# Splitting weights on GpSimd, one run of k times v matmuls, and a new order of issue in a fused mLSTM and MoE kernel

## The chip, the cores and the metric

The kernel runs on one core of a Trainium2 chip. The metric is the device time of one execution in microseconds. Times of a kernel are given as the median of several runs. One execution was taken by the hardware profiler; the rows below are from that one.

## What is computed

Two parts follow one another. The first is an mLSTM layer (4 batches, 8 heads, 768 time steps, head size 40), a recurrence with gates:

```python
m_new = np.maximum(f_gate[:, :, t] + m, i_gate[:, :, t])
f_stab = np.exp(f_gate[:, :, t] + m - m_new)
i_stab = np.exp(i_gate[:, :, t] - m_new)
C = f_stab[:, :, None, None] * C + i_stab[:, :, None, None] * np.einsum('bhd,bhe->bhde', vt, kt)
n = f_stab[:, :, None] * n + i_stab[:, :, None] * kt
h_tilde = np.einsum('bhde,bhe->bhd', C, qt)
denom = np.maximum(np.abs(nq), 1.0)
y[:, :, t] = o * h_tilde / denom
```

Its output, 3072 tokens of 320 values, goes through an MLP with 2048 hidden units: `h = x @ w_in`, `g = h * erf(softplus(h))`, `g @ w_out`. Inputs and output are float32; the two weights reach the chip as 64 bit numbers, of which the kernel makes float32 values itself.

## The kernel before

**Attention.** The sequence is cut into 6 chunks of 128 tokens. A step is one chunk of one batch, so there are 24 steps. Within a step the recurrence is written as matrices: decay factors (`pe`, then `ex` on ScalarE and a triangular select `sel` on GpSimd), scores of q and k (`S`, TensorE), their product `w` (VectorE), the output `ph` from scores, v and the state, and the update of the state: `vg` (v times a decay, VectorE), `pk` (k times `vg`, TensorE, lines 635 to 639), `sa` and `sk` (VectorE, or ScalarE in the first chunk). Heads are held as four pairs; even heads (j = 0) lie on partitions 0 to 39, odd heads (j = 1) on 64 to 103. `pk` is made once for each j, four matmuls each, into a PSUM tile of its own; the last chunk has none, so 20 steps have it. `y` (line 669) is the step's output; its last 64 columns are doubled (line 672) so that three transposes (`tr`) of 128 columns bring tokens onto columns; `xh` and `xl` are its high and low part in the fp32r type that TensorE reads in one pass.

**MLP.** Two batches of a chunk (256 tokens) are a block, and a block has four groups of 512 hidden units, so there are 48 groups. A group has 32 matmuls `up` (line 818), the activation on ScalarE and VectorE over tiles of 128x1024 (`hb`, `a`, `b`, `w` and others), its high and low part `gh` and `gl` (lines 868, 873), and 24 matmuls `dn` (lines 887, 888, 890) into two PSUM banks.

**Weights.** They are decoded in the start of the program, in 26 pieces: 16 of w_out with 320 columns, and 10 of w_in with 512, two of which cover the tail rows. For each, `val` (ScalarE, line 707) and `bits` (VectorE, three instructions, lines 712 to 715) make the float32 value in the tile `bits`, of which there are two, `hi` (ScalarE, line 720) rounds it to the high part, `dif` (TensorE, lines 725 and 726) forms value minus high part in PSUM with an identity and a negative identity, and `lo` (ScalarE, line 730) writes that as the low part.

**What sets the order.** Every piece of work is put into a list with a due time: the time of its unit (a step, a group, a decode) plus an offset from a table by the name of the part. The list is sorted by these numbers and issued in that order, so that each engine gets its instructions in the order of the list. All loads and stores are issued on SP. The tile pools hold few buffers (four PSUM tiles for attention, `dif` among their users), so an instruction also waits for the release of a buffer.

Of the kernel before, what the change touches and what calls it, by code (L numbers as in the profile page):

```python
# [9 lines left out]
F32 = mybir.dt.float32  # L10
F32R = mybir.dt.float32r
# [38 lines left out]
SETUP = {'setup': -653.6399, 'rhs0': -316.5197, 'rhs1': -7.8928, 'sel': -20.425}  # L50
GATE = {'load': -160.6071,
    'scan': -129.7377,
    'g': -118.9644,
    'sum': -85.9459,
    'exp': -69.3145,
    'part0': -64.8632,
    'part1': -57.829,
    'part2': -53.3066,
    'rhs': -44.557}
ATT_FIRST = {'load': -98.3436,  # L60
    'loadv': -167.9076,
    'khi': -0.958,
    'qhi': -84.1108,
    'klo': -36.0204,
    'qlo': -40.8927,
    'stk0': -106.1734,
    'stk1': -42.28,
    'rows': -205.5,
    'pe0': -204.9951,
    'pe1': -84.7223,  # L70
    'ex0': -104.2074,
    'ex1': -80.6796,
    'sel0': -99.9161,
    'sel1': -76.6928,
    'S0': -72.5713,
    'S1': -66.4977,
    'vg0': -86.1606,
    'vg1': -75.2945,
    'w0': -66.7387,
    'w1': -60.3516,  # L80
    'th': -51.6975,
    'pq': -84.6914,
    'qa': -69.7526,
    'ph0': -50.833,
    'ph1': -48.4014,
    'ph2': -41.1641,
    'ph3': -34.4417,
    'pk0': -76.6612,
    'pk1': -43.5318,
    'sa0': -34.523,  # L90
    'sa1': -33.2596,
    'sk0': -75.5148,
    'sk1': -41.374,
    'den': -25.7622,
    'yg': -25.29,
    'y': -21.6911,
    'tr': -15.7542,
    'xh': -3.4201,
    'xl': -0.3588}
ATT_NEXT = {'load': -108.5865,  # L100
    'loadv': -65.7264,
    'khi': -43.9486,
    'qhi': -36.8481,
    'klo': 33.0974,
    'qlo': 4.1048,
    'stk0': -62.7653,
    'stk1': 33.0459,
    'rows': -112.0,
    'pe0': -92.4353,
    'pe1': -82.6231,  # L110
    'ex0': -85.3469,
    'ex1': -74.7973,
    'sel0': -83.8594,
    'sel1': -59.1013,
    'S0': -64.4044,
    'S1': -29.3249,
    'vg0': -46.0099,
    'vg1': -19.402,
    'w0': -39.4592,
    'w1': -14.1493,  # L120
    'th': -41.0893,
    'pq': -109.6295,
    'qa': -38.5364,
    'ph0': -10.0541,
    'ph1': -6.3375,
    'ph2': 5.1946,
    'ph3': 6.4602,
    'pk0': -35.9301,
    'pk1': -7.3506,
# [853 lines left out]
```

## Time and profile before

| | us |
|---|---|
| median of 3 runs | 543.33 |
| lowest and highest run | 537.8, 544.72 |
| the profiled execution | 542.79 |
| its span, first to last instruction | 541.1 |

The span is what the profile can show; 1.7 us of the execution lie outside it. Engines are called PE (TensorE), PEld (its weight loads), DVE (VectorE), ACT (ScalarE), POOL (GpSimd) and SP (which issues DMAs). A row of the instructions in order of time has the start, the duration, engine, line, operation and tiles; matmuls are pipelined, so that durations overlap and the distance from one start to the next is what a matmul costs. An fp32 matmul is recorded as two.

### The profile page before, as it was taken

What the parts mean: (1) busy time and instruction counts of PE and PEld (TensorE: products, weight loads), DVE (VectorE), ACT (ScalarE), POOL (GpSimd) and SP (SyncE); (2) the same over time, 40 slices, a digit from 0 to 9 for tenths busy, and PEclk for the clock granted to TensorE, in tenths of its full rate; (3) what the DMA queues carried; (4) which work ended last, traced back from release to release, by engine and by line L of the source; (5) the groups of instructions that cost most, each with busy time, mean ns of one, the idle gap of its engine ahead of it and who ended that gap; (6) DMA issues with size and microseconds to landing.
All of it is one profiled execution on the core that took longest, in us unless ns stands there. A gap on an engine that the chain in (4) does not pass through costs nothing.

```text
span 541.1 us, 10846 instructions
## 1 busy us (share of the span) xinstructions
PE 521.8 (96%) x4086; PEld 491.9 (91%) x4086; DVE 435.9 (81%) x693; ACT 448.2 (83%) x714; POOL 92.4 (17%) x112
## 2 busy tenths in 40 slices
PE   3989999999899999999999999999999999999997
PEld 2757799899899999999999999999999999999986
DVE  5987899979788878888888898788898678776663
ACT  5776999989868978979878978878979889889993
POOL 3220001312211211211211211211211220200000
PEclk9996999999899999999999999999999999999999
DMA  8996114504504503404513504513504514400000
GB/s 272 276 324 214 40 34 134 153 27 144 150 2 152 165 25 124 150 16 152 155 35 116 157 17 138 166 38 106 167 8 135 162 44 137 140 1 26 0 25 24
DMA packets 28302, 58.85 MB, mean 109 GB/s; under 512 B 4156, under 2 KB 8764, under 8 KB 28252
## 3 DMA queue, kind: packets, MB, share of 16 engines
q1 hardware_dynamic: 28252, 58.18, 34.8%
q8 instruction: 32, 0.52, 0.4%
q14 instruction: 18, 0.15, 0.1%
HBM read 33.40 MB, written 3.93 MB: 69 GB/s over the span
## 4 chain that ended last, share of the span: by engine, by line
PE 84%; DMA 6%; DVE 4%; ACT 3%; issue 1%; SPq 1%; POOL 0%; DVEq 0%; ACTq 0%; POOLq 0%
PE h L818 32%; PE po L887 10%; PE po L890 10%; PE po L888 9%; PE pa L629 7%; DMA n<-in_w_in_dram 4%; PE pa L626 4%; PE pa L586 3%; PE pa L639 3%; PE pa L725 2%; DMA stk<-parts 2%; PE pa L566 2%; PE pa L678 1%; PE pa L589 1%; SPq L554 1%
## 5 line engine op out<-in xcount | busy, mean ns | idle before, releaser
L818 PE MATMUL h<-xh,wh 128*128 128x256 f32 x576 | 160.1, 287 | 0.0
L818 PE MATMUL h<-xl,wh 128*128 128x256 f32 x576 | 157.3, 282 | 0.0
L887 PE MATMUL po<-woh,gh 128*128 128x320 f32 x384 | 122.4, 330 | 2.1 <-ACT o_sb L896 1.3
L888 PE MATMUL po<-wol,gh 128*128 128x320 f32 x384 | 114.9, 310 | 0.0
L818 PEld LDWEIGHTS h<-xh,wh 128*128 128x128 f32 x576 | 109.6, 190 | 1.9 <-issue 1.0
L818 PEld LDWEIGHTS h<-xl,wh 128*128 128x128 f32 x576 | 109.5, 190 | 0.2
L818 PE MATMUL h<-xh,wl 128*128 128x256 f32 x384 | 108.3, 282 | 0.0
L873 DVE TENSOR_TENSOR gl<-hb,gh 128x1024 fp32r<-128x1024 f32 x48 | 59.7, 1243 | 21.8 <-ACT gh L868 16.6
L577 POOL TENSOR_SCALAR_AFFINE_SELECT dm<-dm 128x512 f32<-128x512 f32 x48 | 47.2, 985 | 170.2 <-ACT dm L573 162.2
L887 PEld LDWEIGHTS po<-woh,gh 128*128 128x128 f32 x384 | 72.8, 190 | 2.7 <-ACT o_sb L896 1.6
L868 ACT ACTIVATE gh<-hb 128x1024 fp32r<-128x1024 f32 x48 | 50.9, 1060 | 28.3 <-DVE hb L863 27.8
L888 PEld LDWEIGHTS po<-wol,gh 128*128 128x128 f32 x384 | 72.9, 190 | 0.6
L818 PEld LDWEIGHTS h<-xh,wl 128*128 128x128 f32 x384 | 73.0, 190 | 0.0
L890 PE MATMUL po<-woh,gl 128*128 128x320 f32 x384 | 72.6, 319 | 0.0
L855 DVE SCALAR_TENSOR_TENSOR n<-n,n 128x1024 f32<-128x1024 f32 x48 | 58.7, 1224 | 14.9 <-ACT n L847 12.2
L851 DVE SCALAR_TENSOR_TENSOR n<-n,hb 128x1024 f32<-128x1024 f32 x48 | 61.8, 1288 | 4.3 <-ACT n L842 4.2
L863 DVE SCALAR_TENSOR_TENSOR hb<-n,hb 128x1024 f32<-128x1024 f32 x48 | 58.4, 1217 | 7.6 <-ACT n L859 7.4
L828 ACT ACTIVATE hb<-h 128x512 f32<-128x512 f32 x96 | 57.3, 597 | 6.1 <-PE h L818 3.3
L859 ACT ACTIVATE n<-n 128x1024 f32<-128x1024 f32 x48 | 51.4, 1070 | 11.4 <-DVE n L855 11.3
L890 PEld LDWEIGHTS po<-woh,gl 128*128 128x128 f32 x384 | 58.9, 188 | 1.1
L834 ACT ACTIVATE n<-h 128x512 f32<-128x512 f32 x96 | 57.8, 602 | 0.0
L629 PE MATMUL pa<-kvo,dm 128*128 128x41 f32 x384 | 54.8, 273 | 0.0
(102 smaller groups left out, 896.4 us busy)
## 6 DMA issues: line engine op xcount, KB each, us to landing
stk<-parts SPq DMA_DIRECT2D x120, 160.0 KB
kvo<-in_kvo_dram SPq DMA_DIRECT2D x24, 484.0 KB
parts<-in_w_out_dram SPq DMA_DIRECT2D x5, 960.0 KB
parts<-in_qk_dram SPq DMA_DIRECT2D x20, 208.0 KB
q_t<-in_qk_dram SPq DMA_DIRECT2D x20, 208.0 KB
out_dram<-o_sb SPq DMA_DIRECT2D x24, 160.0 KB
stk<-in_qk_dram SPq DMA_DIRECT2D x4, 416.0 KB
hb<-in_w_in_dram SPq DMA_DIRECT2D x2, 512.0 KB
```

The lines of the kernel that those rows point to most:

```text
L629: nc.tensor.matmul(v.ph[:, 2 * p + j], v.w[j][:, p], v.v1[:, 2 * p + j], start=(c == 0), stop=(c == 0 or j == 1))
L818: nc.tensor.matmul(v.h[n // 2][:, n % 2 * T:(n % 2 + 1) * T], w, m, start=(q == 0), stop=(q == len(ops) - 1))
L828: nc.scalar.activation(v.hb[:, hs], v.h[i], AF.Copy)
L834: nc.scalar.activation(v.a[:, hs], v.h[i], AF.Tanh, scale=PARAMS[0], bias=PARAMS[1])
L851: nc.vector.scalar_tensor_tensor(out=v.a, in0=v.a, scalar=PARAMS[8], in1=v.hb, op0=ALU.add, op1=ALU.mult)
L855: nc.vector.scalar_tensor_tensor(out=v.a, in0=v.a, scalar=PARAMS[9], in1=v.b, op0=ALU.mult, op1=ALU.add)
L859: nc.scalar.activation(v.a, v.a, AF.Tanh, scale=PARAMS[10], bias=PARAMS[11])
L863: nc.vector.scalar_tensor_tensor(out=v.hb, in0=v.a, scalar=1.0, in1=v.hb, op0=ALU.add, op1=ALU.mult)
L873: nc.vector.tensor_tensor(v.gl, v.hb, v.gh.bitcast(F32), op=ALU.subtract)
L887: nc.tensor.matmul(po[k, b], v.gh[:, ts], woh[:, w], start=(j == 0), stop=False)
L888: nc.tensor.matmul(po[k, b], v.gh[:, ts], wol[:, w], start=False, stop=False)
L890: nc.tensor.matmul(po[k, b], v.gl[:, ts], woh[:, w], start=False, stop=(j == NFF - 1))
```

## The change

Four edits:

- `dif` is gone, with the negative identity and one PSUM tile per decode; the low part is a subtraction on GpSimd, from the value and the high part, both in SBUF.
- `pk` is one part instead of two: eight matmuls, even and odd heads in turn, into one PSUM tile. The sums into the state read their rows of it.
- The copy that doubles y's last 64 columns moves from GpSimd to VectorE.
- Nearly all due times have other values. Two lines of the tables as they are now, as an example:

```diff
-    'klo': -21.0673,
+    'klo': -21.0991,
-    'pk0': 6.9497,
-    'pk1': -1.5624,
+    'pk': -0.9185,
```

The code:

```diff
-        nc.scalar.activation(nident, ident, AF.Copy, scale=-1.0)
...
+        if not last:
+
+            @at('pk')
+            def _():
+                v.pk = psum(NPR, V1)
+                for p in range(NPR):
+                    for j in range(2):
+                        nc.tensor.matmul(v.pk[64 * j:64 * j + D, p], v.kn[:, 2 * p + j], v.vg[j][:, p], start=True, stop=True)
+
         for j in range(0 if last else 2):
             js = slice(64 * j, 64 * j + D)
-
-            @at(f'pk{j}')
-            def _(j=j, js=js):
-                v.pk[j] = pk = psum(NPR, V1)
-                for p in range(NPR):
-                    nc.tensor.matmul(pk[js, p], v.kn[:, 2 * p + j], v.vg[j][:, p], start=True, stop=True)
...
-                    nc.scalar.activation(so, v.pk[j][js], AF.Copy)
+                    nc.scalar.activation(so, v.pk[js], AF.Copy)
                 else:
-                    nc.vector.tensor_tensor(so, so, v.pk[j][js], op=ALU.add)
+                    nc.vector.tensor_tensor(so, so, v.pk[js], op=ALU.add)
...
-            nc.gpsimd.tensor_copy(y[:, 320:384], y[:, 256:320])
+            nc.vector.tensor_copy(y[:, 320:384], y[:, 256:320])
...
-        @at('dif')
-        def _():
-            v.z = ps_a.tile([128, 512], F32, name="pa")[:, 0:n]
-            nc.tensor.matmul(v.z, ident, v.val, start=True, stop=False)
-            nc.tensor.matmul(v.z, nident, hi(), start=False, stop=True)
-
         @at('lo')
         def _():
-            nc.scalar.activation(lo(), v.z, AF.Copy)
+            nc.gpsimd.tensor_tensor(lo(), v.val, hi().bitcast(F32), op=ALU.subtract)
```

What the new order does is shown at three places. The first is TensorE ahead of the first `up` matmul. Before, with transposes at line 678, scores at 589, `dif` at 725 and 726, `up` at 818:

```order
L678 MATMUL pa<-ident,kvo 128x128 x3
L589 MATMUL pa<-stk 128x128 x4
L725 MATMUL pa<-bits,ident 128x512
L726 MATMUL pa<-wh,nident 128x512
L589 MATMUL pa<-stk 128x128 x4
L725 MATMUL pa<-bits,ident 128x512
L726 MATMUL pa<-wh,nident 128x512
L818 MATMUL h<-xh,wh 128x256
```

The same place now, where the transposes are line 682, the last decay matmuls 569 and `up` 816:

```order
L569 LDWEIGHTS rhsE_77
L569 MATMUL pa<-splB_83,rhsE_77 128x128
L682 MATMUL pa<-ident,kvo 128x128 x6
L816 MATMUL h<-xh,wh 128x256
L816 MATMUL h<-xl,wh 128x256
```

The eight score matmuls of the third batch, and the decode's, no longer stand between the transposes and the first `up`; the scores come behind the first group of 32 `up` matmuls.

The second place is GpSimd behind its set-up, where line 559 copies decay rows for a batch, 577 is the select and 672 the copy of y. Before:

```order
L559 COPY splB_81<-spl 32x256
L559 COPY splB_82<-spl 32x256
L577 AFFINE_SELECT dm<-dm 128x512 x4
L559 COPY splB_83<-spl 32x256
L559 COPY splB_84<-spl 32x256
L672 COPY kvo<-kvo 128x64
L577 AFFINE_SELECT dm<-dm 128x512 x2
```

Now, with the subtractions at line 728:

```order
L560 COPY splB_80<-spl 32x256
L560 COPY splB_81<-spl 32x256
L728 TENSOR_TENSOR wol<-bits,woh 128x320 x2
L560 COPY splB_82<-spl 32x256
L560 COPY splB_83<-spl 32x256
L728 TENSOR_TENSOR wol<-bits,woh 128x320 x2
L578 AFFINE_SELECT dm<-dm 128x512 x2
L728 TENSOR_TENSOR wol<-bits,woh 128x320
L578 AFFINE_SELECT dm<-dm 128x512 x2
L728 TENSOR_TENSOR wol<-bits,woh 128x320
L728 TENSOR_TENSOR wl<-bits,wh 128x512 x2
```

Four subtractions now stand ahead of the first select, and five ahead of the third and fourth.

The third place is SP's list of loads, where `gt` is the gates of a chunk (here the second chunk's), `parts` raw w_out, and `hb`, `gh`, `gl` and `n` raw w_in. Before:

```order
L748 DMA n_328<-in_w_in_dram 128x1024
L519 DMA stk<-in_qk_dram 104x1024 x2
L748 DMA gh<-in_w_in_dram 128x1024
L775 DMA wh<-stk 64x512 x4
L429 DMA gt<-in_gates_dram 128x2x128
L525 DMA kvo<-in_kvo_dram 128x968 x2
```

Now:

```order
L746 DMA gh<-in_w_in_dram 128x1024
L746 DMA hb<-in_w_in_dram 128x1024
L430 DMA gt<-in_gates_dram 128x2x128
L761 DMA n_286<-in_w_in_dram 64x1024 x2
L786 DMA parts<-in_w_out_dram 128x3x640
L746 DMA n_324<-in_w_in_dram 128x1024
```

The gate load has moved from behind most loads of weights to right behind the first two of w_in.

## Rows read from the trace of the kernel before

**Rows 1.** Busy time of each engine, share of the span, instructions.

```profile
PE 521.8 (96%) x4086; PEld 491.9 (91%) x4086; DVE 435.9 (81%) x693; ACT 448.2 (83%) x714; POOL 92.4 (17%) x112
```

**Rows 2.** Stretches: us, busy us and (instructions) by engine, clock, DMA share, GB/s.

```profile
48.00:60.00 12.00, 12.00 (x76) 9.66 (x75) 8.43 (x19) 9.44 (x20) 0.00 (x0) 0.86 0.23 80
60.00:110.00 50.00, 48.80 (x376) 45.71 (x376) 47.31 (x81) 47.91 (x83) 6.98 (x8) 1.00 0.32 95
...
200.00:300.00 100.00, 100.00 (x828) 97.11 (x827) 84.75 (x138) 83.91 (x129) 18.75 (x19) 1.00 0.34 105
```

**Rows 3.** Groups of instructions: shapes, count | busy us, mean ns | idle before.

```profile
L639 PEld LDWEIGHTS pa<-vg,kvo 128*40 128x40 f32 x320 | 15.3, 117 | 6.9 <-issue 3.6 <-DVE gl L873 0.7 <-DVE dm L600 0.6
L595 DVE TENSOR_TENSOR vg<-kvo,dm 128x164 f32<-128x164 f32 x40 | 14.0, 352 | 0.0
...
L726 PE MATMUL pa<-woh,nident 128*128 128x320 f32 x16 | 8.9, 556 | 0.0
...
L726 PE MATMUL pa<-wh,nident 128*128 128x512 f32 x8 | 7.3, 913 | 0.0
...
L726 PE MATMUL pa<-stk,nident 128*128 128x512 f32 x2 | 1.5, 742 | 0.0
```

**Rows 4.** TensorE in order of time, two decodes between up matmuls.

```profile
51.53 0.70 PE L725 MATMUL pa<-bits,ident 128*128 128x320 f32 x2
...
52.22 0.28 PE L818 MATMUL h<-xh,wh 128*128 128x256 f32 x1
...
60.83 1.02 PE L725 MATMUL pa<-bits,ident 128*128 128x512 f32 x2
...
61.92 0.28 PE L818 MATMUL h<-xh,wh 128*128 128x256 f32 x1
```

**Rows 5.** TensorE: first and last decode ahead of the first up matmul.

```profile
10.37 1.38 PE L725 MATMUL pa<-bits,ident 128*128 128x320 f32 x2
...
45.96 2.07 PE L725 MATMUL pa<-bits,ident 128*128 128x512 f32 x2
...
48.25 0.41 PE L818 MATMUL h<-xh,wh 128*128 128x256 f32 x1
```

**Rows 6.** TensorE: four score matmuls and what follows.

```profile
58.71 1.16 PE L589 MATMUL pa<-stk 40*128 40x128 f32 x8
59.79 0.38 PE L818 MATMUL h<-xh,wh 128*128 128x256 f32 x1
```

**Rows 7.** Waits of VectorE, 0 to 48 us: total, times, longest.

```profile
DVE bits L712 <- ACT bits L707: 4.0, 5, 1.7
DVE m_c L435 <- DMA gt<-in_gates_dram: 3.9, 2, 2.1
```

**Rows 8.** GpSimd in order of time, 35 to 38 us.

```profile
35.10 0.80 POOL L577 TENSOR_SCALAR_AFFINE_SELECT dm<-dm 128x512 f32<-128x512 f32 x1 [0.40 <-ACT dm L573]
37.55 0.24 POOL L672 COPY kvo<-kvo 128x64 f32<-128x64 f32 x1 [1.65 <-DVE kvo L669]
37.73 0.64 POOL L577 TENSOR_SCALAR_AFFINE_SELECT dm<-dm 128x512 f32<-128x512 f32 x1
```

**Rows 9.** VectorE in order of time: beside that select, and the third gl.

```profile
34.91 0.49 DVE L713 SCALAR_TENSOR_TENSOR bits<-parts,bits 128x320 int32<-128x320 int32 x1
35.44 0.80 DVE L715 SCALAR_TENSOR_TENSOR bits<-parts,bits 128x320 int32<-128x320 int32 x1
...
93.90 1.23 DVE L873 TENSOR_TENSOR gl<-hb,gh 128x1024 fp32r<-128x1024 f32 x1 [0.46 <-ACT gh L868]
```

**Rows 10.** TensorE: its first matmul with the third gl.

```profile
96.69 0.45 PE L890 MATMUL po<-woh,gl 128*128 128x320 f32 x2
```

**Rows 11.** TensorE: one run of k times v in the full part.

```profile
236.95 0.50 PE L639 MATMUL pa<-vg,kvo 128*40 128x41 f32 x8
237.38 0.39 PE L818 MATMUL h<-xh,wh 128*128 128x256 f32 x1
```

More of the change, by code (lines that the diff above doesn't have):

```diff
@@ new lines @@
+ATT_FIRST = {'load': -194.0236,
+    'loadv': -144.9749,
+    'khi': -100.2713,
+    'qhi': -211.4726,
+    'klo': 163.9357,
+    'qlo': -275.9474,
+    'stk0': 81.3371,
+    'stk1': -83.5161,
+    'rows': -476.0599,
+    'pe0': -280.2714,
+    'pe1': -282.4843,
+    'ex0': -132.5421,
+    'ex1': -130.7473,
+    'sel0': -114.2683,
+    'sel1': -112.2627,
+    'S0': -104.2892,
+    'S1': -155.9373,
+    'vg0': -91.6484,
+    'vg1': -71.9389,
+    'w0': -78.8353,
+    'w1': -63.5547,
+    'th': -101.0303,
+    'pq': -166.0896,
+    'qa': -53.9067,
+    'ph0': -61.2735,
+    'ph1': -57.7467,
+    'ph2': -52.1923,
+    'ph3': -49.506,
+    'pk': -67.5984,
+    'sa0': 9.8528,
+    'sa1': 170.1622,
+    'sk0': -34.9022,
+    'sk1': -48.2244,
+    'den': -32.091,
+    'yg': -31.3479,
+    'y': -26.0352,
+    'tr': -12.6979,
+    'xh': -9.1723,
+    'xl': 4.6811}
@@ new lines @@
+ATT_NEXT = {'load': -79.7884,
+    'loadv': -66.3845,
+    'khi': -259.972,
+    'qhi': -10.4566,
+    'klo': -5.5541,
+    'qlo': 215.008,
+    'stk0': -13.3658,
+    'stk1': 161.9015,
+    'rows': -211.282,
+    'pe0': -133.8957,
+    'pe1': -106.7482,
+    'ex0': -81.3685,
+    'ex1': -88.9192,
+    'sel0': -70.8477,
+    'sel1': -48.5552,
+    'S0': -30.2817,
+    'S1': -20.3688,
+    'vg0': -34.5805,
+    'vg1': -30.9364,
+    'w0': -26.0142,
+    'w1': -13.3729,
+    'th': -28.6583,
+    'pq': -172.7696,
+    'qa': 34.8793,
+    'ph0': -9.376,
+    'ph1': 3.8853,
+    'ph2': 12.118,
+    'ph3': -2.4117,
+    'pk': -28.0819,
+    'sa0': 3.838,
+    'sa1': 5.5896,
+    'sk0': -17.8822,
+    'sk1': 1.0695,
+    'den': 16.7779,
+    'yg': 23.7691,
+    'y': 25.7755,
+    'tr': 32.7854,
+    'xh': 35.097,
+    'xl': 37.7041}
@@ new lines @@
+ATT = {'load': -49.7161,
+    'loadv': -10.7603,
+    'khi': -26.893,
+    'qhi': -28.5035,
+    'klo': -21.0991,
+    'qlo': -19.5892,
+    'stk0': -17.7322,
+    'stk1': -5.8505,
+    'rows': -37.7933,
+    'pe0': -18.9247,
+    'pe1': -29.6965,
+    'ex0': -17.3222,
+    'ex1': -23.5141,
+    'sel0': -8.757,
+    'sel1': -7.4701,
+    'S0': -6.8558,
+    'S1': -3.1856,
+    'vg0': -4.6086,
+    'vg1': -3.1355,
+    'w0': -2.797,
+    'w1': -2.2748,
+    'th': -4.1275,
+    'pq': -30.4107,
+    'qa': -7.9468,
+    'ph0': -0.3416,
+    'ph1': 6.5295,
+    'ph2': 4.7765,
+    'ph3': 0.0208,
+    'pk': -0.9185,
+    'sa0': 11.8195,
+    'sa1': 19.8995,
+    'sk0': 23.1339,
+    'sk1': 23.4453,
+    'den': 8.3804,
+    'yg': 9.2641,
+    'y': 9.5288,
+    'tr': 14.0382,
+    'xh': 19.2935,
+    'xl': 21.0425}
@@ new lines @@
+MLP = {'up0': 9.2649,
+    'up1': 9.7638,
+    'up2': 11.6838,
+    'up3': 12.7485,
+    'hb0': 14.152,
+    'a0': 13.664,
+    'hb1': 22.0446,
+    'a1': 18.0629,
+    'a2': 22.9056,
+    'sq': 25.872,
+    'b': 27.091,
+    'ah': 29.4165,
+    'ab': 30.409,
+    'w': 35.3503,
+    'wh': 37.2152,
+    'gh': 39.2349,
+    'gl': 42.2437,
+    'dn0': 56.8124,
+    'dn1': 56.924,
+    'dn2': 58.0378,
+    'dn3': 60.5833,
+    'dn4': 58.3883,
+    'dn5': 62.4279,
+    'dn6': 63.1173,
+    'dn7': 63.1469,
+    'o0': 65.0061,
+    'o1': 71.1207}
```

433 lines of the change are left out of this document (147 added, 286 removed).

## Prediction

> **What bounds the kernel now.** I read the page's busy times first, then the table of stretches, then TensorE's instructions in order of time, and last the waits of VectorE and the few places where GpSimd and VectorE work at once. TensorE is busy 96% of the span [rows 1], and 100.00 of 100 us in the middle of the program, where VectorE has 84.75 and ScalarE 83.91 [rows 2]. There nothing but TensorE's own work counts. The start is another matter. From 60 to 110 us TensorE has 48.80 of 50 us, ScalarE 47.91 and VectorE 47.31: three engines are nearly full at once, because the weights are still being decoded there. From 48 to 60 us VectorE has 8.43 of 12 [rows 2]. So work that is taken off TensorE in the start is worth something only as far as the other engines can run ahead with it.
>
> The change touches three things: the decode (26 times, all of it in the start), the matmuls of k times v (20 steps), and one small copy per step (24 steps). Besides, all engines get a new order.
>
> **The decode.** The two matmuls that form the low part leave TensorE. They ran 16 times on 320 columns and 8 + 2 times on 512 [rows 3]. In a dense stretch the time from their start to the start of what follows is 52.22 - 51.53 = 0.69 us for 320 columns and 61.92 - 60.83 = 1.09 us for 512 [rows 4]. In all that is 16 x 0.69 + 10 x 1.09 = 21.9 us of TensorE. But 15 of the 26 (9 small, 6 large; the first at 10.37, the last at 45.96) lie ahead of the first up matmul at 48.25 [rows 5], where TensorE waits on the decode and on attention for its inputs. Behind it lie 11 (7 small, 4 large): 7 x 0.69 + 4 x 1.09 = 9.2 us. The new order also takes the eight score matmuls of the third batch from ahead of the first up group and puts them behind it, at 59.79 - 58.71 = 1.08 us for four [rows 6], so 2.2 us come back. TensorE's own work behind the first up shrinks by 9.2 - 2.2 = 7.0 us.
>
> *When the first up starts.* It needs xl of the second batch, which VectorE writes. VectorE's work ahead of that is nearly the same in the new order: one 512 column decode less, some gate operations more. What can go is its idle time in the first 48 us: 4.0 us in which it waits for the ScalarE step of a decode, and 2.1 us (the longest of the two waits for gates) for the gate load of the second chunk, which SP now issues right behind the first two loads of w_in [rows 7]. ScalarE is relieved of one copy per decode, so I let both go: -6.1 us. Against it stands GpSimd, where four subtractions, each waiting for ScalarE's high part, now stand ahead of the first select, and with it of the first vg of VectorE. And the two engines meet: a select of 0.64 us when alone took 0.80 us beside a decode, and the VectorE instruction that met it took 0.80 in place of the 0.49 us of its neighbour [rows 8, 9]: 0.31 us lost on VectorE for one GpSimd instruction. Fourteen of the new subtractions stand ahead of the second xl; 14 x 0.31 = 4.3 us. First up: 48.25 - 6.1 + 4.3 = 46.45, a gain of 1.8 us. Both ends: 42.15 if the subtractions cost VectorE nothing, 52.6 if no idle time goes and they cost 4.3.
>
> The cost of one subtraction is not in the trace of before. From below it is nothing on VectorE, when it falls into a gap (the select at 37.73 met no VectorE work). From above, two inputs at the select's pace for one, 2 x 0.64 = 1.28 us for 512 columns and 0.80 for 320, all of it lost to VectorE. I take 0.31, the loss that a row shows, for either size.
>
> The Trainium skill is stricter here. SBUF — State Buffer, section "Who interferes with whom", says that a VectorE instruction with two SBUF inputs and a GpSimd instruction that reads SBUF exclude each other for a whole instruction, and that issue order decides who waits. The decode's two bit merges are of this kind, and so are the new subtractions. In the rows the loss is 0.31 of 0.64 us, so about half of an instruction; by the rule in full, each subtraction would cost VectorE its whole length, which is the last rival below.
>
> *Behind the first up.* TensorE could be 7.0 us faster. The tight place is the third group: VectorE writes its gl from 93.90 to 95.13, and TensorE starts on it at 96.69 [rows 9, 10], 1.6 us later. To hand this gl over earlier VectorE has its idle time since 48 us: 12 - 8.43 = 3.6 us, and 35/50 of 50 - 47.31, so 1.9 us [rows 2], with the 1.6 us 7.1 in all. From that go the last 12 subtractions, 12 x 0.31 = 3.7 us, and two of the moved y copies at the 0.24 us that I take for one, 0.5. There remain 7.1 - 4.2 = 2.9 us that TensorE can really gain by the third group; the other 4.1 of its 7.0 become waits for gl. Later VectorE has room again (84.75 of 100) and takes nothing more, but a wait of TensorE does not come back.
>
> **k times v.** Twenty steps, two runs of four matmuls each become one run of eight. A run of four takes 237.38 - 236.95 = 0.43 us [rows 11]. If even and odd heads overlap in TensorE, the run of eight takes 0.43 instead of 0.86, and 20 x 0.43 = 8.6 us go. If on the other hand a weight load shows where it did not (0.117 us each, beside 0.43/8 = 0.054 us per recorded matmul [rows 3, 11]), a step loses 16 x 0.063 = 1.0 us, 20 us in all. The row nearest is the run as it stands, so I take 0 for both: the same matmuls, one behind the other. One PSUM tile less per step, and one less per decode, costs nothing either way while TensorE is full. The run now waits for both vg of its step; the state matmuls, ph and then down matmuls are queued behind it on TensorE, so that a late vg would show as a gap there. With VectorE free for 15 of 100 us I cost this at nothing.
>
> The skill's TensorE: Matmul & The Clock Gate, section "Why this matters for your kernels", has matmuls with few output rows overlap when their outputs start on different groups of partitions, as those of even and odd heads do here. No run shown here has the two side by side; by the rule the sum would be 8.6 us less, the first rival.
>
> **The y copy.** 24 times from GpSimd to VectorE. The nearest VectorE row is 0.352 us for 164 columns [rows 3]; for 64 columns I take the 0.24 us which GpSimd needs for it alone [rows 8], 24 x 0.24 = 5.8 us on VectorE in all, with ends 0 and 24 x 0.352 = 8.4. It is hidden behind TensorE where VectorE has 15 us of 100 free; if that room were gone, it would cost these 5.8 us. The two in the start are in the sum.
>
> **The sum.** Span 541.1 - 1.8 - 2.9 = 536.4 us. The profiled execution took 542.79 us, 1.7 more than its span, and lies 0.5 below the median of 543.33; so 538.1 us. What a measurement of this kernel can tell from no change is about 2%, here 10.9 us, and this forecast is below that.
>
> **Rivals.**
> 1. *The heads overlap.* For it: the two halves write to separate partitions and read separate parts of TensorE's columns. Against it: 0.054 us per matmul is already so short that something other than the array may set it. Time 538.1 - 8.6 = 529.5 us.
> 2. *GpSimd works for nothing, and TensorE keeps all its gain.* For it: GpSimd is busy for 6.98 of 50 us at 60 to 110 [rows 2], and some of its instructions meet no VectorE work [rows 8]. Then the first up starts at 42.15 and all 7.0 us stay: 541.1 - 6.1 - 7.0 + 1.7 = 529.7 us. Against it: VectorE has to be all but full for 60 us.
> 3. *VectorE stands still behind GpSimd.* Place: from the first decode to the third gl. Each subtraction takes its upper price, 10 x 1.28 + 16 x 0.80 = 25.6 us of VectorE. There are 6.1 us of idle time ahead of the first up and 7.1 behind it, 13.2 us; what is over, 12.4 us, delays the third gl and with it all that follows: 541.1 + 12.4 + 1.7 = 555.2 us. It decides from a loss of 13.2/26 = 0.51 us per subtraction; below that the kernel is not slower. For it: the rows at 35 us, and that ScalarE waits for a decode buffer which now GpSimd gives back. Against it: the measured loss is 0.31.
>
> **How the numbers follow.** Forecast (VectorE takes back part, the heads do not overlap): 0.55, its own range 532 to 544. Heads overlap: 0.17. GpSimd for nothing: 0.18. VectorE stands still: 0.10. The first two rivals both lie below the bound of 532.4 us in most of their spread, so faster is 0.85 x 0.35 and 0.03 from the forecast's lower edge, 0.33. Slower than 554.2 us is a little over half of the third rival, 0.06. The rest, 0.61, is no change that could be told. The range leaves out the outer parts of the rivals: 524 to 552 us.
>
> **What would show it.** In the changed kernel's profile: no PE rows with ident beside the transposes, and TensorE about 22 us less busy; first up at 46 or 47 us (42 would speak for rival 2, over 50 for rival 3); GpSimd subtractions of some 0.6 to 1.3 us, and decode instructions of VectorE beside them longer by 0.3; a wait of TensorE for gl or for ScalarE at the second to fourth group, some 4 us together; the run of eight at 0.86 us from its start to what follows (0.45 would be rival 1); TensorE without gaps from 150 us on. The forecast is wrong if the four groups in the full part take another time than before, if a new wait shows up there, or if TensorE's early waits are gone or exceed 10 us.

## The result, and the profile after

The changed kernel takes 543.46 us in the median of 20 runs (541.12 to 544.68), the kernel before 541.07 us in 20 runs beside them (536.57 to 544.72). The ratio is 1.0047, with a 95% interval of 1.0025 to 1.0068: the change makes the kernel slower by 0.2 to 0.7%. Forecast were 538.1 us and a gain. The profiled execution has a span of 542.0 us, against 541.1 before.

That near tie hides two effects of 7 to 8 us each. The first view is the page's busy times; below it stands TensorE's busy share in 40 slices of the span.

```profile
PE 499.1 (92%) x4008; PEld 483.0 (89%) x4008; DVE 451.5 (83%) x717; ACT 438.0 (81%) x687; POOL 85.0 (16%) x114
...
PE   2574798979999999999999999999999999999996
```

TensorE lost 521.8 - 499.1 = 22.7 us of work [rows 1], and the span did not get shorter. What went was filled with idle time, nearly all of it in the first 10 slices. The table of stretches has it in numbers (us, busy us and instructions by engine, clock, DMA share, GB/s):

```profile
48.00:60.00 12.00, 6.89 (x33) 6.46 (x34) 11.57 (x20) 6.34 (x12) 6.67 (x8) 1.00 0.87 249
60.00:110.00 50.00, 42.78 (x314) 40.22 (x315) 46.33 (x73) 41.50 (x73) 16.66 (x14) 0.86 0.28 78
...
200.00:300.00 100.00, 100.00 (x857) 98.25 (x856) 86.69 (x150) 84.57 (x132) 8.65 (x12) 1.00 0.32 95
```

From 48 to 60 us TensorE was full before and VectorE had room, 8.43 of 12 [rows 2]; now VectorE is nearly full with 11.57 and TensorE has 6.89. From 60 to 110 us TensorE falls from 48.80 to 42.78. From 200 to 300 us it is full in both kernels.

Where the two effects part is seen in the first up matmul of a group. These are TensorE's instructions in order of time: in the kernel before the first up of the 16th and the 20th of the 48 groups,

```profile
206.65 0.28 PE L818 MATMUL h<-xh,wh 128*128 128x256 f32 x1
...
247.51 0.28 PE L818 MATMUL h<-xh,wh 128*128 128x256 f32 x1
```

and in the kernel after the first up of all, then one run of k times v and what follows it, and the same two groups:

```profile
50.23 0.58 PE L816 MATMUL h<-xh,wh 128*128 128x256 f32 x1 [2.31 <-ACT xh L691]
...
214.85 0.28 PE L816 MATMUL h<-xh,wh 128*128 128x256 f32 x1
...
235.95 0.51 PE L640 MATMUL pa<-vg,kvo 128*40 128x41 f32 x16
236.39 0.45 PE L627 MATMUL pa<-state,q_t 104*128 104x82 f32 x2
...
254.51 0.28 PE L816 MATMUL h<-xh,wh 128*128 128x256 f32 x1
```

The span falls into three parts, and the three add up:

| | before | after | difference | forecast |
|---|---|---|---|---|
| start to first up [rows 5] | 48.25 | 50.23 | +2.0 | -1.8 |
| first up to the 16th group's first up | 158.40 | 164.62 | +6.2 | -2.9 |
| 16th group's first up to the end | 334.45 | 327.15 | -7.3 | 0 |
| span | 541.1 | 542.0 | +0.9 | -4.7 |

One thing is hidden in the column of the kernel before: TensorE's clock. These are the 10 us from 40 us on, in the kernel before and in one with the same start, but for the copies of y ("The copy of y alone", below), and then the second kernel's first up and its 16th group's:

```profile
40.00:50.00 10.00, 9.93 (x34) 6.54 (x33) 7.67 (x18) 7.29 (x15) 0.64 (x1) 0.56 0.93 290
...
40.00:50.00 10.00, 8.27 (x52) 6.23 (x53) 7.80 (x19) 8.14 (x17) 0.00 (x0) 1.00 0.96 307
...
43.96 0.28 PE L818 MATMUL h<-xh,wh 128*128 128x256 f32 x1
...
203.33 0.28 PE L818 MATMUL h<-xh,wh 128*128 128x256 f32 x1
```

In the kernel before the granted clock was 0.56 there, so that for most of the stretch it stood at the lower of its two levels, 1.2 GHz, while TensorE was busy 9.93 of 10 us; in the 10 us ahead of it TensorE had 7.92 us of work at a clock of 1.00. With 1.00 from 0 to 110 us, the same start is 4.3 us shorter at the first up and 3.3 us at the 16th group. Other times of the kernel before agree: beside the run on SyncE's queue it took 538.24 and 539.28 us at a mean clock of 1.00, and 545.59 at 0.98. That the clock is the whole reason is argued and was not tested by itself. So the loss of the start is 8.2 us against this execution of the kernel before, and 11.5 us (214.85 - 203.33) against one at the upper level, 2.4 GHz.

**The loss.** Two rows of GpSimd show two of the new subtractions,

```profile
38.73 1.27 POOL L728 TENSOR_TENSOR stk<-bits,stk 128x512 fp32r<-128x512 f32 x1 [1.29 <-ACT stk L724]
43.10 1.59 POOL L728 TENSOR_TENSOR wl<-bits,wh 128x512 fp32r<-128x512 f32 x1 [3.10 <-ACT wh L724]
```

and VectorE's rows of the same time show what they met:

```profile
38.73 1.61 DVE L673 TENSOR_TENSOR kvo<-kvo,den 128x320 f32<-128x320 f32 x1
...
43.08 0.49 DVE L717 SCALAR_TENSOR_TENSOR bits<-parts,bits 128x320 int32<-128x320 int32 x1
43.60 1.44 DVE L719 SCALAR_TENSOR_TENSOR bits<-parts,bits 128x320 int32<-128x320 int32 x1
...
45.40 0.49 DVE L673 TENSOR_TENSOR kvo<-kvo,den 128x320 f32<-128x320 f32 x1
```

The product of y takes 0.49 us at 45.40 and 1.61 us at 38.73, where it starts together with a subtraction of 1.27: VectorE is kept for 1.12 us, nearly the whole subtraction. At 43.60 it is 1.44 against the 0.49 of its neighbour, 0.95 lost: the subtraction there ends at 44.69, so it had 1.09 us left. Read so over all 26 subtractions, 27 instructions of VectorE that read nothing from PSUM start while one runs, and in 24 of them the loss is what the subtraction still has to run, less 0.14 us (within 0.02). The 21 that were already running are not lengthened, like the one at 43.08, and the subtraction can be longer for it, 1.59 in place of 1.27. Three that read PSUM, as `dm<-pa,dm`, are not lengthened either. What this does to groups of instructions is seen in VectorE's groups of the first 140 us, by shape (count, busy us, mean ns), of the kernel before and then of the kernel after:

```profile
L712 DVE TENSOR_SCALAR bits<-bits 128x320 int32<-128x320 int32 x16 | 5.6, 351 | 2.4 <-ACT bits L707 2.4
...
L713 DVE SCALAR_TENSOR_TENSOR bits<-n,bits 128x512 int32<-128x512 int32 x4 | 2.8, 692 | 0.1
```

```profile
L716 DVE TENSOR_SCALAR bits<-bits 128x320 int32<-128x320 int32 x16 | 7.9, 497 | 4.8 <-ACT bits L711 4.7
...
L717 DVE SCALAR_TENSOR_TENSOR bits<-n,bits 128x512 int32<-128x512 int32 x4 | 4.3, 1069 | 0.1
```

The instructions and their counts are the same; only the means grew, from 351 to 497 ns and from 692 to 1069. Taken over all of VectorE's instructions of the first 140 us, each against the lowest mean that its kind has in any of these kernels, the excess is about 3.6 us before (beside GpSimd's selects and copies) and 16.0 after. The change thus costs VectorE some 12.4 us, 0.48 for each of the 26 subtractions. Counted in the 27 rows alone, against what their kinds take where GpSimd stands still, it is about 15 us, 0.58 each; GpSimd's selects cost VectorE less than before.

Whom it holds up is read from the stretches between first ups, first to second and second to sixth group, of the kernel before and then of the kernel after:

```profile
48.25:59.79 11.54, 11.54 (x74) 9.30 (x72) 7.97 (x17) 9.10 (x20) 0.00 (x0) 0.87 0.21 75
59.79:100.73 40.94, 39.74 (x298) 36.90 (x298) 38.32 (x66) 39.90 (x72) 4.65 (x6) 1.00 0.31 91
```

```profile
50.23:70.37 20.14, 13.85 (x88) 12.48 (x88) 19.56 (x33) 12.57 (x23) 9.15 (x9) 0.80 0.41 126
70.37:110.59 40.22, 36.41 (x263) 34.78 (x262) 36.56 (x56) 34.41 (x59) 13.83 (x12) 0.93 0.36 99
```

Between the first two groups VectorE is now busy 19.56 of 20.14 us, with 33 instructions where 17 stood before: the new order has put work of the third and fourth batch there. TensorE waits, and its clock is at 0.80. Its waits from 8 to 145 us (total, times, longest) end on VectorE for the most part, but for one of 9.2 us for GpSimd's copies of decay rows, which was there before with 8.7:

```profile
PE pa L640 <- DVE dm L601: 5.3, 1, 5.3
PE h L816 <- DVE xl L695: 3.9, 2, 2.9
PE pa L640 <- issue: 3.1, 1, 3.1
PE pa L630 <- DVE dm L601: 2.7, 1, 2.7
```

**The gain.** The run of k times v, now eight matmuls in place of four, takes 236.39 - 235.95 = 0.44 us to what follows, nearly as long as a run of four took before [rows 11]. From the 16th to the 20th group it is 254.51 - 214.85 = 39.66 us, where it was 247.51 - 206.65 = 40.86. The forecast had said that a changed time of these four groups would show it wrong.

### The profile page after: what moved, and what is told of

Read it like the earlier page. It is cut to its first block, busy times and chain, and to the rows that moved or that the text cites. A ratio compares the mean times of both kernels' runs of the same rounds, so it can differ in the third digit from the quotient of the medians.

```text
span 542.0 us, 10517 instructions
## 1 busy us (share of the span) xinstructions
PE 499.1 (92%) x4008; PEld 483.0 (89%) x4008; DVE 451.5 (83%) x717; ACT 438.0 (81%) x687; POOL 85.0 (16%) x114
## 4 chain that ended last, share of the span: by engine, by line
PE 70%; DVE 17%; ACT 6%; issue 3%; DMA 2%; SPq 1%; DVEq 0%; ACTq 0%
PE h L816 28%; PE po L885 9%; PE po L888 9%; PE po L886 8%; PE pa L630 5%; PE pa L627 3%; PE pa L587 3%; DVE bits L717 3%; DVE bits L719 3%; DVE bits L716 2%; DVE hb L861 2%; DVE n L853 1%; PE pa L567 1%; PE pa L640 1%; DMA parts<-in_w_out_dram 1%
## 5 line engine op out<-in xcount | busy, mean ns | idle before, releaser
L816 PE MATMUL h<-xh,wh 128*128 128x256 f32 x576 | 168.8, 299 | 3.4 <-ACT xh L691 2.3
L816 PE MATMUL h<-xl,wh 128*128 128x256 f32 x576 | 160.8, 285 | 3.9 <-DVE xl L695 3.9
L885 PE MATMUL po<-woh,gh 128*128 128x320 f32 x384 | 119.5, 321 | 1.5 <-ACT gh L866 1.5
L816 PEld LDWEIGHTS h<-xl,wh 128*128 128x128 f32 x576 | 111.2, 193 | 5.2 <-DVE xl L695 4.5
L816 PEld LDWEIGHTS h<-xh,wh 128*128 128x128 f32 x576 | 111.4, 193 | 4.5 <-ACT xh L691 2.7
L888 PE MATMUL po<-woh,gl 128*128 128x320 f32 x384 | 82.9, 319 | 0.0
L578 POOL TENSOR_SCALAR_AFFINE_SELECT dm<-dm 128x512 f32<-128x512 f32 x48 | 33.4, 718 | 301.5 <-ACT dm L574 173.6
L888 PEld LDWEIGHTS po<-woh,gl 128*128 128x128 f32 x384 | 61.9, 189 | 0.4
L849 DVE SCALAR_TENSOR_TENSOR n<-n,hb 128x1024 f32<-128x1024 f32 x48 | 59.2, 1234 | 3.1 <-ACT n L840 3.1
L630 PE MATMUL pa<-kvo,dm 128*128 128x41 f32 x384 | 57.7, 284 | 3.1 <-DVE dm L601 2.7
```

Of the source, the lines that this page charges most:

```text
L630: nc.tensor.matmul(v.ph[:, 2 * p + j], v.w[j][:, p], v.v1[:, 2 * p + j], start=(c == 0), stop=(c == 0 or j == 1))
L816: nc.tensor.matmul(v.h[n // 2][:, n % 2 * T:(n % 2 + 1) * T], w, m, start=(q == 0), stop=(q == len(ops) - 1))
L849: nc.vector.scalar_tensor_tensor(out=v.a, in0=v.a, scalar=PARAMS[8], in1=v.hb, op0=ALU.add, op1=ALU.mult)
L885: nc.tensor.matmul(po[k, b], v.gh[:, ts], woh[:, w], start=(j == 0), stop=False)
L888: nc.tensor.matmul(po[k, b], v.gl[:, ts], woh[:, w], start=False, stop=(j == NFF - 1))
```

## The experiments

Two theories of the slow start stood against each other at first. Theory A: VectorE stands still while GpSimd subtracts, and this is the time that the start lacks. Theory B: the low halves come later from GpSimd than from TensorE and ScalarE, and what waits for them is late, whatever VectorE does. Later came C, SyncE's queue. TensorE's clock is a fourth candidate; the runs for the other three settle it too. For the full part the question was whether the overlap of the heads makes the gain, or the order.

### The decode alone

The kernel before, in its own order, with the subtraction on GpSimd:

```diff
-        @at('dif')
...
-            nc.scalar.activation(lo(), v.z, AF.Copy)
+            nc.gpsimd.tensor_tensor(lo(), v.val, hi().bitcast(F32), op=ALU.subtract)
```

> The kernel before with one edit: the low part is subtracted on GpSimd, in the old order; the 52 matmuls and 26 ScalarE copies of it are gone. Theory A (each subtraction holds VectorE for most of its length, 0.3 to 1.0 us): VectorE loses 10 to 15 us in the start, the first up starts no earlier than 48 us and the 16th group's first up (206.65 before) lies at 206 to 212 us; time 541 to 546. Theory B (the new order of issue made the start late, not the subtractions): the start gains from TensorE's 22 us less work, the 16th group's first up at 199 to 202, time 533 to 537.

Measured: 552.47 us, ratio to before 1.0228 (1.0196 to 1.0259). The 16th group's first up:

```profile
216.88 0.28 PE L812 MATMUL h<-xh,wh 128*128 128x256 f32 x1
```

That is 10.2 us later than before, and from there to the end of the span of 551.1 us it takes 334.2 us, as before. So this one edit makes the start late, in the old order too, and by more than I had expected. VectorE's excess is about 18.3 us. That is not all that changed. The next decode's value needs one of the two tiles `bits`, which now GpSimd gives back, and ScalarE waits for it (first 145 us):

```profile
ACT bits L707 <- POOL wol L724: 11.2, 9, 1.8
ACT bits L707 <- POOL wl L724: 8.8, 7, 3.3
```

How the 10.2 us divide between VectorE's lost time and these 20 us of waits is open here. In the kernel after the same waits come to 2.7 us.

### k times v alone

The kernel before with one run in place of two, at places of my own in the old order:

```diff
-    'pk0': 6.9497,
-    'pk1': -1.5624,
+    'pk': -1.5624,
...
+                    for j in range(2):
+                        nc.tensor.matmul(v.pk[64 * j:64 * j + D, p], v.kn[:, 2 * p + j], v.vg[j][:, p], start=True, stop=True)
```

> The kernel before with one edit: k times v of even and odd heads in turn in one run of eight into one bank (and the sums into the state put close behind it). Theory A and B alike: the run of eight takes 0.44 us from start to start as in the changed kernel, four groups of the full part take about 39.6 to 39.9 us instead of 40.85, and the time falls by 8 to 10 us to 531 to 533. If the gain of the full part comes from the new order instead, the time stays within 2 us of 541.

Measured: 537.74 us, ratio 0.9942 (0.9913 to 0.9971): faster, by less than expected. The run itself takes 0.44 us here too (271.08 to 271.52). From the 16th group's first up to the end it takes 333.2 us, 1.2 less than before; TensorE's busy time in this stretch, the first number behind its length, falls by 4.2 (kernel before, then this one):

```profile
206.65:541.09 334.44, 329.07 (x2659) 321.06 (x2657) 263.80 (x386) 279.94 (x423) 53.87 (x56) 1.00 0.29 91
...
206.74:539.97 333.23, 324.87 (x2659) 316.88 (x2657) 265.24 (x388) 279.04 (x424) 57.19 (x56) 1.00 0.30 91
```

The other 3.0 are lost in new waits; TensorE's from 206 us to the end:

```profile
PE pa L678 <- POOL kvo L672: 2.2, 6, 0.4
...
PE pa L583 <- DMA stk<-parts: 0.8, 3, 0.3
```

The kernel before has neither in this stretch. The transposes, now earlier on TensorE, meet GpSimd's copy of y. The matmuls are cheaper, but the order around them has to fit.

### The subtraction cut to 8 columns

The kernel after, the rest of the low half filled with zeros, so that the low part of the weights is left out but for 8 columns of each piece:

```diff
-            nc.gpsimd.tensor_tensor(lo(), v.val, hi().bitcast(F32), op=ALU.subtract)
+            nc.gpsimd.memset(lo()[:, 8:n].bitcast(F32), 0.0)
+            nc.gpsimd.tensor_tensor(lo()[:, 0:8], v.val[:, 0:8], hi().bitcast(F32)[:, 0:8], op=ALU.subtract)
```

> The changed kernel, but GpSimd reads only 8 of the 320 or 512 columns of each subtraction and fills the others with zeros by a write that reads nothing; so the waits between engines stay and most of the reading beside VectorE is left out (the low part of the weights is left out with it). Theory A: VectorE's decode instructions are back at 0.49 and 0.69 us, the 16th group's first up comes from 214.85 to 203 to 207 us, time 532 to 537. Theory B: the start stays within 3 us, time 540 to 544.

Measured: 533.3 us, ratio to before 0.9875 (0.9826 to 0.9925). Its first up and the 16th group's:

```profile
44.82 0.58 PE L817 MATMUL h<-xh,wh 128*128 128x256 f32 x1 [1.57 <-ACT xh L691]
...
203.60 0.28 PE L817 MATMUL h<-xh,wh 128*128 128x256 f32 x1
```

Up to the 16th group's first up it is 11.25 us shorter than the kernel after, and the rest is the same (530.8 - 203.60 = 327.2). But this cuts the lock and GpSimd's delay together, so it does not yet tell A from B.

### As late, but without reading

The kernel after, again with 8 columns subtracted, and then filled twice, so that GpSimd is busy as long as with the whole subtraction and the low half is as late:

```diff
-            nc.gpsimd.tensor_tensor(lo(), v.val, hi().bitcast(F32), op=ALU.subtract)
+            nc.gpsimd.tensor_tensor(lo()[:, 0:8], v.val[:, 0:8], hi().bitcast(F32)[:, 0:8], op=ALU.subtract)
+            for _ in range(2):
+                nc.gpsimd.memset(lo()[:, 8:n].bitcast(F32), 0.0)
```

> The kernel after, with GpSimd kept as long as in it between a high half and the release of its low half, by instructions that read nothing: the subtraction takes 8 columns alone, and two fills with zeros of the other columns stand behind it (together some 0.9 us for 320 columns and 1.2 to 1.5 us for 512, where the whole subtraction takes 1.04 and 1.41). The low part of all weights but 8 columns of each piece is left out. Theory A (the start is late because VectorE stands still while GpSimd subtracts): VectorE's instructions over words keep their short times (0.53 us for 320 columns in the shortened kernel, 0.58 in the kernel after), and the time is that of the shortened subtraction: 531 to 536 us. Theory B (the start is late because low halves come later, whoever else runs): 541 to 546 us, as the kernel after.

Measured: 534.15 us, ratio 0.9856 (0.9806 to 0.9907). VectorE's groups and GpSimd's, first 140 us, and then a fill and the VectorE instruction that starts beside it:

```profile
L716 DVE TENSOR_SCALAR bits<-bits 128x320 int32<-128x320 int32 x16 | 5.5, 346 | 4.5 <-ACT bits L711 4.5
...
L717 DVE SCALAR_TENSOR_TENSOR bits<-n,bits 128x512 int32<-128x512 int32 x4 | 2.8, 692 | 0.1
...
L730 POOL MEMSET wol<- 128x312 f32 x32 | 11.8, 368 | 0.9
L730 POOL MEMSET wl<- 128x504 f32 x16 | 8.7, 546 | 0.5
...
25.96 1.25 POOL L730 MEMSET wl<- 128x504 f32 x2
...
26.14 0.62 DVE L716 TENSOR_SCALAR bits<-bits 128x512 int32<-128x512 int32 x1 [0.18 <-ACT bits L711]
```

GpSimd's decode instructions take 31.9 us here with the short subtractions and the tail's, 30.7 in the kernel after, and VectorE's means are back at 346 and 692 ns. Theory B is out as the main cause: the low halves are as late as in the kernel after, and some 10 us of the time are gone (0.9856 against 1.0047 of 541 us). The clock is out as the main cause too: it was 0.57 from 60 to 70 us here, 0.61 in the kernel after, and yet the loss is gone.

Three reservations. In the profiled executions the 16th group's first up is at 206.67 here and at 203.60 with 8 columns alone, though the medians are 0.85 us apart; lateness may cost some of these 3 us. Fills are not free: the shift of words, with one operand, takes 0.62 us at 26.14, where it takes 0.42 alone (at 40.49 in the kernel after), though the merges with two operands stay at 692 ns. And the tile `bits` is given back sooner here, since the 8 columns are subtracted first: ScalarE doesn't wait for it at all, so the 2.7 us of these waits in the kernel after went together with VectorE's loss.

### The subtraction on VectorE

The kernel after, with the low half made by VectorE, right behind the high half:

```diff
-    'lo': 23.7245}
+    'lo': 15.42}
...
-            nc.gpsimd.tensor_tensor(lo(), v.val, hi().bitcast(F32), op=ALU.subtract)
+            nc.vector.tensor_tensor(lo(), v.val, hi().bitcast(F32), op=ALU.subtract)
```

> The kernel after with the subtraction of the low half on VectorE in place of GpSimd, issued right behind the high half. VectorE's own price by its rows over two operands in SBUF is about 0.48 us for 320 columns and 0.69 for 512, 16 x 0.48 + 10 x 0.69 = 14.6 us in all, against some 12 to 15 us that it now loses beside GpSimd. Theory A (VectorE's time is what the start lacks): 541 to 548 us, since VectorE pays about the same, and its instructions over words are short again. Theory B (the lateness of GpSimd's low halves is what counts): the low halves come 0.4 to 0.9 us sooner each, 533 to 539 us.

Measured: 545.0 us, ratio 1.0063 (1.0028 to 1.0097), the same as the kernel after. VectorE's new groups:

```profile
L728 DVE TENSOR_TENSOR wol<-bits,woh 128x320 fp32r<-128x320 f32 x16 | 7.9, 491 | 7.1 <-ACT woh L724 6.9
...
L728 DVE TENSOR_TENSOR wl<-bits,wh 128x512 fp32r<-128x512 f32 x8 | 5.4, 687 | 2.1 <-ACT wh L724 2.1
```

With the two tail pieces (1.4 us) VectorE pays 14.7 us of its own, and its excess falls to about 2.2 us, 16.9 in all against 16.0 in the kernel after. Moving the subtraction to GpSimd saves VectorE next to nothing. Here no tile `bits` waits for GpSimd, and the time is the same: VectorE's time is what the start lacks.

### Even heads first, then odd

The kernel after, its eight matmuls in another order, in the same run and bank:

```diff
-                for p in range(NPR):
-                    for j in range(2):
+                for j in range(2):
+                    for p in range(NPR):
```

> The changed kernel with one edit: in the run of eight first the four matmuls of the even heads, then the four of the odd heads, same bank. If it is the alternation between the two halves of TensorE's columns that lets them overlap, the run takes 0.8 to 0.87 us instead of 0.44 and the time rises by 7 to 9 us, to 550 to 553. If a longer run into one bank is enough, the run stays at 0.44 to 0.5 us and the time within 1.5 us of 543.5.

Measured: 544.92 us, ratio 1.0088 (1.0054 to 1.0121). One run:

```profile
236.09 0.69 PE L640 MATMUL pa<-vg,kvo 128*40 128x41 f32 x16
236.71 0.45 PE L627 MATMUL pa<-state,q_t 104*128 104x82 f32 x2
```

A run now takes 0.62 us. So of the 0.42 us by which one run in turn (0.44) is shorter than two runs of four (0.86), 0.18 come from the turn of heads and 0.24 from one run in place of two. In 20 runs the turn is worth 3.6 us at most, half of it behind the 16th group, where the stretch to the end is 2.0 us longer than in the kernel after. That lies between the two expectations: the turn counts, but less than the one run.

### SyncE's queue

A third theory, C: in the kernel after SyncE stands from 24.6 to 38.67 us for the tail's low half, and the loads of the third and fourth batch are queued behind. Here its four copies go out behind those loads:

```diff
-            if done:
+
+        if done:
+            @unit(-19.0 if name == ('t', 0) else DECODE[name], DEC if name != ('t', 0) else dict(done=0.0))('done')
+            def _():
                 done()
```

> The kernel after, with the four copies of the tail's halves into wh (which SyncE sends from 38.67 us on, after standing since 24.6 us for the tail's low half) sent behind the loads of the third and fourth batch's rows and values. Theory A (VectorE's lost time beside GpSimd is the cause of the late start): VectorE is busy from 30 to 70 us in any case; within 1.5 us of the kernel after, 542 to 545, though the loads come some 10 us sooner. Rival C (SyncE's stand is what makes the start late, by the late rows and values of the third and fourth batch): 536 to 540 us, with the third and fourth batch's k times v some 4 us sooner.

Measured: 542.86 us, ratio 1.0028 (0.9998 to 1.0059). SyncE's queue in order of time:

```profile
28.38 0.34 SPq L521 DMA_DIRECT2D stk<-in_qk_dram  x1
44.15 3.79 SPq L527 DMA_DIRECT2D kvo<-in_kvo_dram  x2
48.03 2.46 SPq L777 DMA_DIRECT2D wh<-stk  x4
```

The rows came 16 us sooner (28.38, against 44.26 in the kernel after), the values hardly (44.15 against 44.87). TensorE's waits for VectorE are the same 5.3, 3.9 and 2.7 us, the 16th group's first up is at 214.91. SyncE's stand for the rows was not the cause. The values were not brought forward by this, so their part stays open.

This execution also says something of the clock. From 20 to 50 us it was at its lower level throughout (0.50), with TensorE busy 16.82 of 30 us; in the kernel after it was 1.00 there:

```profile
20.00:50.00 30.00, 16.82 (x102) 13.69 (x101) 27.85 (x50) 14.86 (x33) 12.93 (x13) 0.50 0.75 223
```

The 16th group's first up is at the same place, 214.91 against 214.85. Where TensorE waits for others, half the clock cost nothing that shows.

### The copy of y alone

The kernel before with that copy on VectorE:

```diff
-            nc.gpsimd.tensor_copy(y[:, 320:384], y[:, 256:320])
+            nc.vector.tensor_copy(y[:, 320:384], y[:, 256:320])
```

> The kernel before with one edit: the copy of y's last 64 columns on VectorE in place of GpSimd. VectorE takes 24 x 0.2 us more over the whole span, and the transposes' release comes from VectorE, without GpSimd's 0.24 us and the hand-over. If it is hidden, as the prediction had it: 539 to 543 us by the profiled time of before (541), within 0.4% of it. If VectorE's added time lies on the path: 544 to 546. If the hand-over was on the path: 536 to 538.

Measured: 539.61 us, ratio 0.9974 (0.9935 to 1.0013): no difference that can be told, as the prediction had it.

### The start of before, the full part of after

The two effects seem to be separate. So: the kernel before with its own decode and its own order for the first four steps and groups, one run of k times v, y's copy on VectorE, and from the fifth step and group on the kernel after's order.

```diff
...
-GROUP_EVERY = 13.6151
-STEP_BEFORE = (26.1425, 14.2715)
+GROUP_EVERY = 13.4771
+STEP_BEFORE = (26.1612, 12.0928)
...
```

> The kernel before in its start (its decode with the difference on TensorE, its order of issue for the first four steps and groups), and the kernel after in the full part: its order of issue from the fifth step and group on, one run for k times v, y's copy on VectorE. Theory: the two effects are separate, the start of before reaches the 16th group's first up product at 206 to 208 us, and from there the full part of after takes 327 us: 533 to 535 us, faster than both by 1 to 1.6%. Rival (the full part's gain needs the start's order, or VectorE becomes the bound from 140 us on): 538 us or more.

Measured: 534.55 us, ratio 0.9862 (0.9819 to 0.9906). The 16th group's first up is at 207.12 us and from there to the end it takes 327.3: both effects stand alone, as expected. TensorE's longest wait from 60 to 110 us shows the seam between the two orders:

```profile
PE pa L563 <- DMA q_t<-in_qk_dram: 5.6, 1, 5.6
```

### The seam closed

The same with the second chunk's gates handled sooner, by 20 of the order's units and, in a second kernel, by 40:

```diff
-CHUNK_AT = {0: -505.6204, 1: 114.7873}
+CHUNK_AT = {0: -505.6204, 1: 95.0}
```

> The mixed kernel, with the second set of gates handled 20 of the order's units sooner. In the mixed kernel TensorE stands still for 5.56 us at 94.08 us, at the first exponent product of the fifth step, whose last wait is for the rows of the gates that SyncE sends at 84.4 to 92.7 us behind other loads. Theory: that wait is the seam of the two orders, it was lost to TensorE for good, and without it the time falls by 3 to 6 us, to 529 to 532. Rival (the span from 60 to 110 us is bound by VectorE and ScalarE, so that the wait goes to another place): 533 to 536, as the mixed kernel.

> The same with the second set of gates 40 units sooner in place of 20. If 20 were enough: the same as that kernel within 0.4%. VectorE's work for the gates (three scans, eight others, some 5 us) then comes ahead of the first groups' work, where VectorE is 95% busy: if that is on the path, 2 to 4 us slower than with 20.

Measured: 531.2 us, ratio 0.9818 (0.9783 to 0.9853), and 531.12 us, ratio 0.9812 (0.9778 to 0.9846). In the second none of TensorE's waits from 60 to 110 us is longer than this one:

```profile
PE pa L563 <- ACT dm L570: 0.4, 1, 0.4
```

The wait of 5.6 us is gone, and 2 to 3 us of it reached the end, less than the 3 to 6 expected. 40 units are as good as 20. These two are the fastest kernels of the study, 1.8 to 1.9% below the kernel before and some 2.3% below the kernel after (0.9812 / 1.0047).

Side by side, in us of the profiled executions (excess: VectorE's, first 140 us, as above). The profiled execution of k times v alone took 542.0 us, 4.3 more than its median, so only its last column counts.

| kernel | excess | first up | 16th group's first up | from there to the end |
|---|---|---|---|---|
| before | 3.6 | 48.25 | 206.65 | 334.4 |
| after | 16.0 | 50.23 | 214.85 | 327.2 |
| decode alone | 18.3 | 50.89 | 216.88 | 334.2 |
| k times v alone | not taken | 49.02 | 206.74 | 333.2 |
| copy of y alone, full clock in the start | not taken | 43.96 | 203.33 | 334.2 |
| 8 columns | 2.9 | 44.82 | 203.60 | 327.2 |
| as late, without reading | 4.2 | 45.27 | 206.67 | 327.2 |
| subtraction on VectorE | 2.2 and 14.7 of its own | 48.34 | 216.47 | 327.2 |
| even heads first | not taken | 49.99 | 214.95 | 329.2 |
| start of before, rest of after | 2.2 | 48.26 | 207.12 | 327.3 |

## Why the prediction was wrong

**What bounds the kernel.** Right in the main: in the start VectorE decides what a gain of TensorE is worth, and from 200 us on TensorE's own work counts. The table above bears both out. But k times v alone shows that waits of TensorE can come up there too, 3.0 us of them.

**The price of a subtraction** is the step that failed first: "I take 0.31, the loss that a row shows, for either size." It is 0.48 on average as the net of the change, 0.58 counted in the rows, 1.12 in the row at 38.73. The row that I took it from [rows 8, 9] obeys the same sum as the others: the select there runs from 35.10 to 35.90, the VectorE instruction starts at 35.44, and of the 0.46 us left 0.31 were lost. I read it as the price of one GpSimd instruction, "about half", where it was the rest of one that had begun 0.34 us earlier. The new subtractions are longer (0.85 and 1.27 us), and VectorE, nearly full, mostly has an instruction that starts early in one. What holds the mean below the whole length is that some VectorE instructions are already running, and that reads of PSUM are not lengthened (the product `dm<-pa,dm` has a mean of 0.68 us in both kernels).

The Trainium skill had the rule, in SBUF — State Buffer, "Who interferes with whom": two SBUF inputs on VectorE against a GpSimd instruction that reads SBUF, and not one that only writes, with the shared port held by one alone. For instructions with two operands the rows agree in both halves: 1.61 us for 0.49 beside a subtraction, 692 ns beside fills. I gave this the 0.10 of the third rival. Its place, the start, is where the loss lies, and the 0.51 which it named as the point of decision lies between the 0.48 and the 0.58 measured; the whole length, 25.6 us of VectorE, was too much.

**The first up.** Forecast 46.45, measured 50.23. With 8 columns subtracted it comes at 44.82, so 5.4 us go with the subtractions ahead of it, where I had put 14 x 0.31 = 4.3. That the 6.1 us of idle time went is not shown: the 48.25 that I started from held some 4 us of the lower clock, and with the full clock the old start reaches its first up at 43.96. The sign was in my own rows, a decode of 2.07 us at 45.96 beside one of 1.02 at 60.83 [rows 4, 5]; I passed over it. The bounds of 42.15 to 52.6 held the measured time.

**Behind the first up.** "There remain 7.1 - 4.2 = 2.9 us that TensorE can really gain by the third group" failed, by 9.1 us, and not through the price alone: with 8 columns subtracted, the stretch to the 16th group is 158.78 us, no shorter than the 158.40 before (159.37 with the copy of y alone). I had sought the tight place at the third gl. It lies between the first and second group, where the new order has 33 VectorE instructions in place of 17. I had counted what was moved there on TensorE (2.2 us of score matmuls), and not on VectorE. Up to the 16th group TensorE's own work did shrink, from 155.4 us busy to 150.4, but its idle time grew from 3.0 to 14.2 us, over the 10 that I had named as a sign of a wrong forecast.

**k times v.** "I take 0 for both" failed: the heads overlap, and a run of eight takes 0.44 us. The first rival, held at 0.17, had 20 x 0.43 = 8.6 us for it. The rows give 20 x 0.42 = 8.4 us of TensorE's work; no run shows the whole of it as time. From the 16th group's first up to the end ten of the runs are left, and there TensorE is busy 329.1 us in the kernel before, 324.9 with k times v alone and 322.9 in the kernel after,

```profile
214.85:542.04 327.19, 322.85 (x2659) 317.72 (x2657) 266.44 (x407) 280.27 (x423) 27.29 (x40) 1.00 0.31 91
```

so of the 7.3 us gained 4.2 are k times v (ten times 0.42), 2.0 less work of TensorE in the new order, and 1.1 less waiting. The upper bound, weight loads that show, did not come. Over eight groups of the full part the kernel before takes 81.86 us and the kernel after 79.30; k times v has 3.44 and 1.76 of these, and the other 0.9 lie in which matmul follows which (the products with the state, for one, went from 3.87 to 3.52 for the same 32 recorded matmuls). The part of the order, 3.1 us in all, I had put at nothing.

**The y copy** was hidden; it takes 0.218 us on VectorE on average, where I had estimated 0.24.

**The sum** came out near the truth, 538.1 against 543.46 and inside the range, by luck, because two errors of opposite sign met: the start is 8.2 us later in place of 4.7 earlier, the full part 7.3 shorter in place of unchanged. The signs given for a wrong forecast were the right ones: first up over 50, eight matmuls in 0.45, another time of the four groups.

Left open: how much of the start the new order costs by itself, since the old decode in the new order was not tried, and how much of the loss goes by ScalarE's 2.7 us of waits for the tile `bits`.

## What to carry to other kernels

Work moved to GpSimd is not free for VectorE: look at what the new instruction reads, and at what VectorE does beside it. A loss seen in one row is not the price of an instruction: set it against what GpSimd's instruction still had to run, and where VectorE is nearly full count the whole length of the new one as the upper bound. Where a change has an effect in two parts of a program, place a mark in the trace (here the first up of a late group) and take the parts apart, and look at TensorE's clock in each before you set two executions side by side: a kernel that is no faster may hold a gain and a loss, and the gain can be kept alone. Here matmuls of 40 output rows that alternate between two halves of the output partitions cost next to nothing beyond those of one half, and one run in place of two was a gain of its own. It became time only in an order that had no new waits for it.

## What the runs showed of the hardware

- A GpSimd subtraction of 512 columns from two operands in SBUF takes 1.27 us, of 320 columns 0.85 to 0.86, where no VectorE instruction is ahead of it, and up to 1.59 and 1.52 otherwise. A VectorE instruction that starts while it runs and reads nothing from PSUM is lengthened by what is left of it, less 0.14 us (24 of 27 rows); one that is already running is not (21 of 21).
- Not only VectorE's instructions with two operands grew: the shift of words, with one, had a mean of 497 in place of 351 ns for 320 columns. It grew beside GpSimd fills too, 0.62 for 0.42 us at 26.14; the merges with two operands did not (692 ns).
- TensorE's clock at its lower level cost some 3 to 4 us where TensorE was nearly full (0.56 from 40 to 50 us, kernel before against the copy of y alone) and nothing that shows where it waited (0.50 from 20 to 50 us, SyncE's queue against the kernel after).
- Eight fp32 matmuls of 40 output rows and 41 columns take 0.44 us when they alternate between output partitions 0 and 64, 0.62 us half by half, and two separate runs of four 2 x 0.43.
